# First three tiles' attention in float32, and the weights' words put together in PSUM

## The chip, the core and the metric

The kernel runs on one core of one Trainium2 chip. A core has five engines with a queue of instructions each: TensorE (PE) multiplies matrices, from SBUF into PSUM; VectorE (DVE), ScalarE (ACT) and GpSimd (POOL) work element by element; SyncE (SP) issues the DMA transfers between HBM and SBUF, and here also the DMA transposes within SBUF. Each engine's queue is laid down when the kernel is built, and an instruction waits on semaphores where it needs what another engine makes. The metric is the time on the device of one launch, in microseconds (us), lower is better.

## What is computed

A block of local and global attention, a gated feed-forward layer, and a soft mixture of eight experts, all on 3072 tokens. Inputs come as float32, except the weights `w_in` and `w_out` of the feed-forward layer, which the kernel receives as 64-bit words (float64) and turns into floating point of its own.

```python
scores = scale * np.matmul(q, k.transpose(0, 1, 3, 2))      # (4, 8, 768, 64)
keep = is_global | is_local                                  # 8 first keys, 96 last
scores = np.where(keep, scores + bias, -1e9)
a = softmax(scores)                                          # over the keys
x = np.matmul(a, v)           # -> (3072, 512)
h = x @ w_in                  # w_in (512, 2048)
x = (h * sigmoid(h)) @ w_out  # w_out (2048, 512)
...                           # soft mixture of experts on x, with phi, w1, w2
```

## The kernel before

The 3072 tokens are 24 tiles of 128, and three tiles make one of eight chunks. Precision is kept with float16 pairs: a float32 operand becomes a high part (`hi`, line 189) and a low part (`lo`, line 197), and a product takes three float16 matmuls, high by high, high by low and low by high. Making these parts is work for ScalarE, VectorE and GpSimd; strings such as `HE`, `PHE`, `PLE`, `L3E`, `LOE` say which engine makes which.

*Attention of a tile T.* `load` (line 240) brings q, k and v into a staging area; tiles 0 to 5 hold two heads on the 128 partitions (`paired`). `split` (line 247) makes the float16 parts of q, k and v; k and v go into rings of four tiles, `kr` and `v16`, and the global keys and values are kept in `kg` and `vg`. `s_step(T, pr)` (line 272) does the scores of two heads: the matmuls (line 293) into the banks `bS`, bias and row maximum on VectorE (line 298), exp on ScalarE (line 299). Every second step finishes half of the heads: the probabilities are split into two float16 parts (lines 312 and 313) and turned by a DMA transpose (line 314), or, for the last half of tile 2, turned by TensorE and split on the way out of PSUM (`flip`, line 208; string `PTE`). `pv_step` (line 324) multiplies them by v (line 336), divides by the row sums (line 346) and puts the transposed output into `xt`, the input of the feed-forward layer.

*Weights.* `w_ahead` (line 407) issues sixteen loads of 1 MB, eight for `w_in` and eight for `w_out`, each into a place (`place`) that is free, some held back by `GATE` until a certain half of the attention is done. `conv(p)` (line 414) turns such a piece into float16 parts, with the 64-bit word's low half as the place of the result. On VectorE line 421 takes the bits that show whether an exponent lies out of range; two TensorE matmuls with a one-column result (line 423) collect them in the bank `bM`. ScalarE (line 428) or GpSimd (line 426) turns one byte of the exponent into a 16-bit piece, VectorE adds the sign (line 429) and moves the fraction in (line 430). ScalarE makes the high part (line 440), and VectorE (line 448) or, for five pieces, ScalarE and GpSimd (lines 443 and 446) the low part. The staged place is then free for the next load.

*Feed-forward.* `l1_step(c, f)` (line 453) does a sixteenth of the hidden layer for chunk c: twelve matmuls (lines 460 to 462), tanh on ScalarE (line 464), the product on VectorE (line 466), and the two parts of the result. `l2_part` (line 475) does the second layer (lines 480 to 482), `l2_end` and `logits` what follows it. Both take their PSUM banks in turn from the four of `bW`.

*Order.* The program writes the attention of tiles 0 to 2 first (`first_items`), with conversion 0 after its fourth item (`START`). Then come the chunks: chunk 0 runs sixteen steps of the first layer, each pair of them behind one conversion of `w_in`, then eight conversions of `w_out`, each followed by its matmuls. Between these steps the attention of the next three tiles is put in (`other_items`), a share after each step. From this text a scheduler of the language makes each engine's queue, so that an operation can stand ahead of others that were written before it. Chunks 1 to 7 need no conversions.

Of the kernel before, what the change touches and what calls it, by code (L numbers as in the profile page):

```python
# [45 lines left out]
def p2(e):  # L46
    return float(2.0 ** e)
# [39 lines left out]
L3E = 'AAPPPAAAAAPAAAAA'  # L87
LOE = 'PVVPVVPVVPPVVVVV'
# [3 lines left out]
PTE = 'DDDDDA'  # L92
# [8 lines left out]
def fast_kernel(tc, keepp, q_l, k_l, v_l, q_f, k_f, n_global, n_local, w_in, w_out, phi, w1, w2, shapes, pick_c, out):  # L101
# [8 lines left out]
    with ExitStack() as ctx:  # L110
# [8 lines left out]
        bank = [psp.tile([128, 512], F32, name=f"bank{i}") for i in range(8)]  # L119
# [8 lines left out]
        one16 = ar.new([2], BF16)  # L128
# [53 lines left out]
        pt = [ar.new([2, 4, 2, 128], F16) for _ in range(2)]  # L182
        psum_ = [ar.new([H], F32) for _ in range(2)]
# [24 lines left out]
        def flip(hi_out, lo_out, in_, eng):  # L208

            for i in range(0, hi_out.shape[1], 4):  # L210
                tb = bW[flips[0] % 4]
# [27 lines left out]

        def load(T, bufs):  # L240
            if paired(T):
                bufs = [bufs[0][:, 0:4], bufs[1][:, 0:4], bufs[2]]
            for s, src in zip(bufs, (q_f, k_f, v_l) if paired(T) else (q_l, k_l, v_l)):
                nc.sync.dma_start(out=s, in_=src[T])
            staged[T] = bufs

        def split(T):
            qs, ks, vs = staged.pop(T)
# [3 lines left out]
            qd = q16[T % 2]  # L252
            n = 4 if paired(T) else 8
            if paired(T):
                qh, ql, qf = qd[:, 0:4], qd[:, 4:8], qs
            else:
                qh, ql, qf = qd, qd[64:128], qs[64:128]
            hi(he, qh, qs, E_QK)
            lo("P" if le == "P" else "V", ql, qf, E_QK, qh if paired(T) else ql)
            hi(he, kr[:, 0, 0:n, u], ks, E_QK)  # L260
            lo("V" if le == "V" else "P", kr[:, 1, 0:n, u], ks, E_QK, kr[:, 0, 0:n, u])
            v3 = vs.rearrange("p (h d) -> p h d", h=H)
            hi(he, v16[:, u, :, 0], v3, E_V)
            lo("V", v16[:, u, :, 1], v3, E_V, v16[:, u, :, 0])
            if t == 0:
                hi("P", kg[:, :, 0:n], kr[:, :, 0:n, u, 0:8], 0)
            if T == 0:
                hi("P", vg[0:8], v16[0:8, u], 0)
# [3 lines left out]
        def s_step(T, pr):  # L272
# [8 lines left out]
            if t == 0 and T < C0 and PTE[2 * T + half] != "D":  # L281
                pfb = pfb.rearrange("p h c -> p (h c)")[:, 0:512].rearrange("p (h c) -> p h c", h=4)
            qd = q16[T % 2]
            for i in range(2):
                h, r, terms = (pr, slice(64 * i, 64 * i + 64), ((0, 0), (0, 1), (1, 0))) if paired(T) else (2 * pr + i, slice(0, 128), ((0, 0), (0, 1)))
                for j, (y, z) in enumerate(terms):
# [938 lines left out]
```

## Time and profile before

| | |
|---|---|
| Median of 3 runs | 766.43 us (765.55 to 767.75) |
| The profiled execution | 765.0 us, of which the span of the profile is 763.2 us |
| TensorE busy | 683.0 us, 89% of the span |
| VectorE busy | 489.0 us, 64% |
| ScalarE busy | 336.6 us, 44% |
| GpSimd busy | 324.7 us, 43% |
| Mean granted TensorE clock | 0.964 |

All rows that follow come from that one profiled execution. A row of a group of instructions gives the line of the program, the engine, the operation, what it writes and reads, shapes and types, how many there are, then the busy time in us and the mean of one in ns, and then the idle time of the engine in front of them with what ended it. An instruction counts as busy from its start to its end, also where it is held up within. A line can be that of a helper: line 191 is any `hi` on ScalarE, lines 199 and 201 any `lo`. The names arena and rows are regions of SBUF, bank is PSUM.

### The profile page before, as it was taken

To read this page: it belongs to the slowest core of one execution; us is meant where nothing else is said; L and a number is where in the kernel's file an instruction comes from. 1 tells how busy PE (TensorE), PEld (TensorE's weight loads), DVE (VectorE), ACT (ScalarE), POOL (GpSimd) and SP (SyncE) were. 2 spreads that over 40 slices of the span, in tenths; PEclk is the share of its full clock that TensorE was granted. 3 is DMA by queue.
4 is the path that set the end of the run, shared out by engine and by line. 5 is a ranking of instruction groups with operands and counts; after the bars stand their busy time and mean duration, and the time that the engine had idled before them with its cause. 6 is when DMAs were issued, how large, how long until landed. Compare 5 with 4: busy or idle time off the path is not lost.

```text
span 763.2 us, 14337 instructions
## 1 busy us (share of the span) xinstructions
PE 683.0 (89%) x5559; PEld 395.0 (52%) x5559; DVE 489.0 (64%) x1108; ACT 336.6 (44%) x855; POOL 324.7 (43%) x267
## 2 busy tenths in 40 slices
PE   2477757598999999999999999999999999998995
PEld 1244423244655565556556654665466546665375
DVE  6999999997775487548735873597266306505232
ACT  7756786553552255245423542454156305303122
POOL 4689684733455356415633673337324320101000
PEclk9978969799999999999999999999999999999997
DMA  6787645565456355733563567354532694295987
GB/s 237 194 249 205 218 87 152 191 181 120 75 125 139 83 113 137 174 75 77 132 138 74 107 137 167 56 111 109 86 43 43 150 320 178 97 357 214 391 330 223
DMA packets 162747, 120.22 MB, mean 158 GB/s; under 512 B 137456, under 2 KB 147184, under 8 KB 156656
## 3 DMA queue, kind: packets, MB, share of 16 engines
q1 hardware_dynamic: 162672, 119.23, 58.4%
q8 instruction: 45, 0.74, 0.4%
q14 instruction: 30, 0.25, 0.1%
HBM read 79.10 MB, written 6.29 MB: 112 GB/s over the span
## 4 chain that ended last, share of the span: by engine, by line
PE 67%; DVE 16%; issue 5%; POOL 4%; DMA 4%; ACT 3%; SPq 0%; ACTq 0%; DVEq 0%; POOLq 0%
PE bank L480 8%; PE bank L481 8%; PE bank L482 8%; PE bank L460 8%; PE bank L462 8%; PE bank L461 8%; PE bank L293 4%; PE bank L336 3%; DVE arena L201 2%; DMA arena<-arena 2%; DVE arena L199 2%; POOL arena L193 2%; PE bank L864 2%; DVE arena L429 2%; PE bank L902 2%
## 5 line engine op out<-in xcount | busy, mean ns | idle before, releaser
L193 POOL TENSOR_SCALAR arena<-arena 128x1024 f16<-128x1024 f32 (+5 forms) x146 | 144.4, 1002 | 237.0 <-ACT arena L299 102.5
L460 PE MATMUL bank<-rows,arena 128*128 128x384 f16 x512 | 168.4, 330 | 6.2 <-ACT arena L191 4.0
L462 PE MATMUL bank<-rows,arena 128*128 128x384 f16 x512 | 168.3, 329 | 0.8 <-DVE arena L448 0.8
L461 PE MATMUL bank<-rows,arena 128*128 128x384 f16 x512 | 168.3, 329 | 0.0
L191 ACT ACTIVATE arena<-bank 128x384 f16<-128x384 f32 (+2 forms) x165 | 81.8, 505 | 177.0 <-DVE bank L466 98.7
L199 POOL TENSOR_TENSOR arena<-arena 128x1024 f16<-128x1024 f32 (+2 forms) x69 | 131.0, 1900 | 41.3 <-ACT arena L191 37.3
L299 ACT ACTIVATE arena<-arena 128x256 f32<-128x256 f32 (+1 forms) x192 | 92.2, 482 | 98.2 <-DVE arena L298 95.3
L481 PE MATMUL bank<-arena 128*128 128x512 f16 x336 | 128.9, 384 | 2.7 <-POOL arena L446 1.9
L480 PE MATMUL bank<-arena 128*128 128x512 f16 x336 | 129.1, 384 | 1.5 <-DVE arena L201 1.5
L482 PE MATMUL bank<-arena 128*128 128x512 f16 x336 | 128.7, 383 | 0.0
L201 DVE SCALAR_TENSOR_TENSOR arena<-bank,arena 128x384 f16<-128x384 f32 (+2 forms) x142 | 81.3, 572 | 32.7 <-ACT arena L191 32.0
L293 PE MATMUL bank<-arena 128*128 128x256 f16 (+3 forms) x432 | 63.4, 288 | 41.5 <-DVE arena L298 23.9
L298 DVE CUSTOM_DVE_ANT_0 arena<-bank,arena 128x256 f32<-128x256 f32 (+1 forms) x192 | 70.5, 395 | 44.2 <-PE bank L293 42.8
L466 DVE SCALAR_TENSOR_TENSOR bank<-arena,bank 128x384 f32<-128x384 f32 x128 | 71.2, 557 | 31.0 <-ACT arena L464 29.8
L199 DVE TENSOR_TENSOR arena<-arena 128x1024 f16<-128x1024 f32 (+2 forms) x50 | 74.7, 1496 | 12.6 <-POOL arena L193 12.2
L464 ACT ACTIVATE arena<-bank 128x384 f32<-128x384 f32 x128 | 61.9, 484 | 21.1 <-PE bank L462 20.8
L293 PEld LDWEIGHTS <-arena 128*128 128x128 f16 (+1 forms) x432 | 36.3, 101 | 66.5 <-issue 38.1
L462 PEld LDWEIGHTS <-arena 128*128 128x128 f16 x512 | 50.4, 99 | 35.4 <-issue 1.6
L461 PEld LDWEIGHTS <-arena 128*128 128x128 f16 x512 | 50.4, 98 | 34.5 <-issue 7.2
L460 PEld LDWEIGHTS <-arena 128*128 128x128 f16 x512 | 50.5, 99 | 31.4 <-issue 2.9
L482 PEld LDWEIGHTS <-arena 128*128 128x128 f16 x336 | 33.1, 99 | 43.9 <-issue 5.3
L480 PEld LDWEIGHTS <-arena 128*128 128x128 f16 x336 | 33.2, 99 | 38.1 <-issue 4.8
(174 smaller groups left out, 808.8 us busy)
## 6 DMA issues: line engine op xcount, KB each, us to landing
arena<-in_w_dram SPq DMA_DIRECT2D x31, 1024.0 KB, 7.4
arena<-in_q_l_dram SPq DMA_DIRECT2D x18, 512.0 KB, 3.7
arena<-in_k_l_dram SPq DMA_DIRECT2D x18, 512.0 KB, 4.0
arena<-in_w_in_dram SPq DMA_DIRECT2D x8, 1024.0 KB, 5.7
arena<-in_w_out_dram SPq DMA_DIRECT2D x8, 1024.0 KB, 4.9
arena<-in_v_l_dram SPq DMA_DIRECT2D x24, 256.0 KB, 3.0
out_dram<-arena SPq DMA_DIRECT2D x4, 768.0 KB, 7.6
out_dram<-arena SPq DMA_DIRECT2D x8, 384.0 KB, 5.0
```

Of the source, the lines that this page charges most:

```text
L191: A.activation(out=out, in_=in_, func=AF.Copy, scale=p2(e))
L193: G.tensor_scalar(out=out, in0=in_, scalar1=p2(e), scalar2=0.0, op0=ALU.mult, op1=ALU.add)
L199: (V if eng == "V" else G).tensor_tensor(out=out, in0=in_, in1=h, op=ALU.subtract)
L201: V.scalar_tensor_tensor(out=out, in0=in_, scalar=p2(e), in1=h, op0=ALU.mult, op1=ALU.subtract)
L293: mm(sp[i][:, :w] if t == 0 else sp[i].rearrange("p (s c) -> p s c", s=2), qd[r, 4 * y + h], kv, start=(j == 0), stop=(j == len(terms) - 1))
L299: A.activation(out=pw, in_=pw, func=AF.Exp, scale=-1.0, bias=nmx[:, T, h:h + 1], accum_out=psum_[T % 2][:, h:h + 1])
L460: mm(hp, wh, x[:, 0, k], start=(k == 0), stop=False)
L461: mm(hp, wh, x[:, 1, k], start=False, stop=False)
L462: mm(hp, wl, x[:, 0, k], start=False, stop=(k == 3))
L480: mm(op, gh, woh[:, f, 0], start=(f == 0), stop=False)
L481: mm(op, gh, woh[:, f, 1], start=False, stop=False)
L482: mm(op, gl, woh[:, f, 0], start=False, stop=(f == 15))
```

## The change

Six edits that belong together:

- Tiles 0 to 5 keep q and k as float32 (`kr32` and `q32` lie where the float16 parts lay). k is loaded in two halves of 64 columns straight into the ring, q into a buffer of its own. `split` no longer makes parts of q and k for these tiles, and each head's scores are one float32 matmul in place of three.
- Tiles 0 to 2 keep v as float32 too, and their probabilities: TensorE transposes these in blocks of 128, four to a bank, and ScalarE copies each bank to SBUF (`p32`). The output takes one float32 matmul a block. The DMA transposes of probabilities of these tiles are gone. Only tile 2's v and, for tile 0, eight rows of v are still split, for what later tiles read of them.
- Two banks of PSUM, one of the four of `bW` and `bM`, become one region `bC` of 1024 columns. In `conv` ScalarE writes the exponent's piece there as whole 32-bit words, for all sixteen pieces; VectorE puts sign and fraction in by two operations on it; ScalarE and VectorE take the two float16 parts from it, for all pieces.
- The exponent check's bits are gathered in SBUF by one VectorE operation a piece, and reduced at the end by two; the 32 matmuls are gone.
- The place of a raw piece counts as free, and the next load is issued, ahead of the two float16 parts.
- Chunk 0 takes its banks for both layers, and the transposes of tiles 0 to 2 theirs, from three of `bW`. The load of tile T + 2, for tile 5, is written after the last scores of tile 3.

The diff, cut to its core:

```diff
-L3E = 'AAPPPAAAAAPAAAAA'
-LOE = 'PVVPVVPVVPPVVVVV'
-PTE = 'DDDDDA'
+PTE = 'A'
-        bank = [psp.tile([128, 512], F32, name=f"bank{i}") for i in range(8)]
+        bank = [psp.tile([128, 512], F32, name=f"bank{i}") for i in range(6)]
+        bC = psp.tile([128, 1024], F32, name="words")
+        bank += [bC[:, 0:512], bC[:, 512:1024]]
...
         def load(T, bufs):
             if paired(T):
-                bufs = [bufs[0][:, 0:4], bufs[1][:, 0:4], bufs[2]]
+                nc.sync.dma_start(out=q_of(T), in_=q_f[T])
+                for z in range(2):
+                    nc.sync.dma_start(out=kr32[:, z, 0:4, T % NR], in_=k_f[T][:, :, 64 * z:64 * z + 64])
+                nc.sync.dma_start(out=v32[T].rearrange("p h d -> p (h d)") if T < C0 else v_next, in_=v_l[T])
+                return
...
             if paired(T):
-                qh, ql, qf = qd[:, 0:4], qd[:, 4:8], qs
+                v3 = v32[T] if T < C0 else v_next.rearrange("p (h d) -> p h d", h=H)
+                if T == 0:
+                    hi("P", kg32, kr32[:, 0, 0:4, u, 0:8], 0)
+                    hi("A", vg[0:8, :, 0], v3[0:8], E_V)
+                    lo("V", vg[0:8, :, 1], v3[0:8], E_V, vg[0:8, :, 0])
+                elif T >= C0 - 1:
+                    hi(he, v16[:, u, :, 0], v3, E_V)
+                    lo("V", v16[:, u, :, 1], v3, E_V, v16[:, u, :, 0])
...
+                if paired(T):
+                    r = slice(64 * i, 64 * i + 64)
...
+                    mm(so, q_of(T)[r, pr], kv, start=True, stop=True)
+                    continue
...
-                if T < C0 and PTE[2 * T + half] != "D":
-                    n = w // 32
-                    flip(ptb[:, 0:n], ptb[:, n:2 * n], pfb.rearrange("p h c -> p (h c)"), PTE[2 * T + half])
-                    held = ptb[:, 2 * n - 1, 127:128]
+                if T < C0:
+                    p32, src = pt32[half], pfb.rearrange("p h c -> p (h c)")
+                    for i in range(0, w // 32, 4):
+                        tb = bW[flips[0] % 3]
+                        flips[0] += 1
+                        for j in range(4):
+                            tr(tb[:, 128 * j:128 * j + 128], src[:, 128 * (i + j):128 * (i + j) + 128], ident)
+                        cp = PTE[flips[0] % len(PTE)]
+                        (A.copy if cp == "A" else V.tensor_copy)(out=p32[:, 128 * i:128 * i + 512], in_=tb)
...
+                if T < C0:
+                    nb = len(blocks)
+                    for s in range(nb):
+                        i = 128 * (nb * hh + s)
+                        mm(o[:, h], pt32[half][:, i:i + 128], v32[T - (nb - 1) + s][:, h], start=(s == 0), stop=(s == nb - 1))
+                    continue
...
-            V.tensor_scalar(out=odd16.bitcast(U16), in0=u16[:, :, 3], scalar1=0x7000, scalar2=0x3000, op0=ALU.bitwise_and, op1=ALU.bitwise_xor)
-            for j in range(2):
-                mm(bM[0:1], one16[:, 0:1], odd16[:, 512 * j:512 * j + 512], start=(p + j == 0), stop=(p + j == 16))
-            if L3E[p] == "P":
-                G.tensor_scalar(out=u16[:, :, 0], in0=by[:, :, 3], scalar1=1.0 / 32, scalar2=-0.484375, op0=ALU.mult, op1=ALU.add)
-            else:
-                A.activation(out=u16[:, :, 0], in_=by[:, :, 3], func=AF.Copy, scale=1.0 / 32, bias=-0.484375)
-            V.tensor_scalar(out=u16[:, :, 1], in0=u16[:, :, 3], scalar1=0x8000, scalar2=None, op0=ALU.bitwise_and)
-            V.scalar_tensor_tensor(out=low, in0=high, scalar=3, in1=low, op0=ALU.logical_shift_left, op1=ALU.bitwise_xor)
+            V.scalar_tensor_tensor(out=odd16, in0=u16[:, :, 3], scalar=0x3000, in1=odd16, op0=ALU.bitwise_xor, op1=ALU.bitwise_or)
+            word = bC.bitcast(I32)
+            A.activation(out=word, in_=by[:, :, 3], func=AF.Copy, scale=1.0 / 32, bias=-0.484375)
+            V.scalar_tensor_tensor(out=word, in0=high, scalar=-(2 ** 31), in1=word, op0=ALU.bitwise_and, op1=ALU.bitwise_xor)
+            V.scalar_tensor_tensor(out=word, in0=high, scalar=3, in1=word, op0=ALU.logical_shift_left, op1=ALU.bitwise_xor)
+            holder[place[p]] = None
+            w_ahead()
...
             A.activation(out=dst[0], in_=src, func=AF.Copy, scale=-p2(e - 128))
-            if LOE[p] != "V":
...
-            else:
-                V.scalar_tensor_tensor(out=dst[1], in0=src, scalar=-p2(e - 128), in1=dst[0], op0=ALU.mult, op1=ALU.subtract)
-            holder[place[p]] = None
-            w_ahead()
+            V.scalar_tensor_tensor(out=dst[1], in0=src, scalar=-p2(e - 128), in1=dst[0], op0=ALU.mult, op1=ALU.subtract)
...
-            hp = bW[turn[0] % 4][:, :n]
+            hp = bW[f % 3 if c == 0 else turn[0] % 4][:, :n]
...
-            op = bW[(turn[0] + m) % 4]
+            op = bW[(m + 1) % 3 if c == 0 else (turn[0] + m) % 4]
...
-                V.memset(odd, 0.0)
-                V.tensor_reduce(out=odd[0:1], in_=bM[0:1], axis=AX.X, op=ALU.max)
+                V.tensor_scalar(out=odd16, in0=odd16, scalar1=0x7000, scalar2=None, op0=ALU.bitwise_and)
+                V.tensor_reduce(out=odd, in_=odd16, axis=AX.X, op=ALU.max)
```

## Rows read from the trace of the kernel before

**Rows 1.** Busy by stretch: length, PE, PEld, DVE, ACT, POOL, clock, DMA share, GB/s

```profile
0.00:57.00 57.00, 29.02 (x237) 15.71 (x237) 48.28 (x115) 37.50 (x93) 37.24 (x43) 0.93 0.78 226
57.00:177.00 120.00, 86.86 (x553) 42.09 (x553) 116.62 (x149) 76.29 (x128) 77.77 (x48) 0.87 0.61 172
177.00:700.00 523.00, 515.49 (x4093) 303.98 (x4091) 302.92 (x787) 209.19 (x602) 206.13 (x171) 1.00 0.53 127
```

**Rows 2.** What VectorE waited for, 57 to 177 us: total, times, longest

```profile
DVE arena L298 <- POOL arena L193: 1.1, 1, 1.1
DVE arena L298 <- PE bank L293: 0.9, 1, 0.9
DVE arena L199 <- POOL arena L193: 0.7, 1, 0.7
```

**Rows 3.** Groups of VectorE by line and shape, 57 to 177 us

```profile
L430 DVE SCALAR_TENSOR_TENSOR arena<-arena 128x1024 int32<-128x1024 int32 x14 | 25.2, 1806 | 0.0
L429 DVE TENSOR_SCALAR arena<-arena 128x1024 uint16<-128x1024 uint16 x13 | 21.8, 1709 | 0.0
L448 DVE SCALAR_TENSOR_TENSOR arena<-arena 128x1024 f16<-128x1024 f32 x10 | 18.0, 1796 | 0.0
L421 DVE TENSOR_SCALAR arena<-arena 128x1024 uint16<-128x1024 uint16 x13 | 12.3, 945 | 0.0
L199 DVE TENSOR_TENSOR arena<-arena 128x1024 f16<-128x1024 f32 x6 | 11.9, 1991 | 0.7 <-POOL arena L193 0.7
...
L199 DVE TENSOR_TENSOR arena<-arena 128x512 f16<-128x512 f32 x3 | 2.0, 679 | 0.0
```

**Rows 4.** Single lines of VectorE, 0 to 190 us: shortest, median, longest in ns

```profile
L466 DVE SCALAR_TENSOR_TENSOR bank<-arena,bank x18: 547/549/556, 68.7 to 188.7; 128x384 f32<-128x384 f32 x18
L201 DVE SCALAR_TENSOR_TENSOR arena<-bank,arena x9: 543/546/692, 81.0 to 190.0; 128x384 f16<-128x384 f32 x6, 128x512 f16<-128x512 f32 x3
L430 DVE SCALAR_TENSOR_TENSOR arena<-arena x16: 1170/1770/4234, 23.4 to 170.4; 128x1024 int32<-128x1024 int32 x16
L429 DVE TENSOR_SCALAR arena<-arena x16: 1297/1525/3229, 21.8 to 168.7; 128x1024 uint16<-128x1024 uint16 x16
L421 DVE TENSOR_SCALAR arena<-arena x16: 643/690/2361, 16.2 to 174.7; 128x1024 uint16<-128x1024 uint16 x16
```

**Rows 5.** Groups of VectorE by line and shape, 0 to 57 us

```profile
L199 DVE TENSOR_TENSOR arena<-arena 128x512 f16<-128x512 f32 x7 | 6.9, 1012 | 0.1
...
L195 DVE TENSOR_SCALAR arena<-arena 128x512 f16<-128x512 f32 x3 | 3.8, 1279 | 0.0
...
L199 DVE TENSOR_TENSOR arena<-arena 128x1024 f16<-128x1024 f32 x2 | 2.4, 1214 | 0.0
```

**Rows 6.** Chain of work, 0 to 60 us: start us, us, what

```profile
28.92 2.61 DVE arena L201
...
32.73 5.53 DMA arena<-arena
```

**Rows 7.** Groups of ScalarE by line and shape, 0 to 177 us

```profile
L428 ACT ACTIVATE arena<-arena 128x1024 uint16<-128x1024 uint8 x12 | 30.0, 2499 | 0.4 <-DMA arena<-in_w_out_dram 0.4
...
L440 ACT ACTIVATE arena<-arena 128x1024 f16<-128x1024 f32 x16 | 18.4, 1148 | 28.1 <-DVE arena L430 26.5 <-DVE arena L448 1.6
```

**Rows 8.** Timeline of TensorE: start us, us, what (float16, then float32)

```profile
34.37 0.83 PE L293 MATMUL bank<-arena 64*128 64x256 f16 x6
...
732.98 1.13 PE L906 MATMUL bank<-arena 128*128 128x256 f32 x4
```

**Rows 9.** SP's queue, one issue; and the page's DMA issues, time to landing

```profile
2.14 0.43 SPq L244 DMA_DIRECT2D arena<-in_q_f_dram  x1
...
arena<-in_q_l_dram SPq DMA_DIRECT2D x18, 512.0 KB, 3.7
```

**Rows 10.** Line 440, once a round: its sixteen, and that of conversion 2

```profile
L440 ACT ACTIVATE arena<-arena x16: 1116/1145/1202, 25.3 to 172.7; 128x1024 f16<-128x1024 f32 x16
...
57.65 1.12 ACT L440 ACTIVATE arena<-arena 128x1024 f16<-128x1024 f32 x1
```

## What I predict

> **What bounds the kernel now.** I read the busy times of the engines by stretches of the span first [rows 1]. From 177 to 700 us TensorE is busy 515 of 523 us at full clock: whatever that train of matmuls starts earlier, the end comes earlier. So the question is what decides when it starts. Between 57 and 177 us VectorE is busy 116.6 of 120 us, TensorE 86.9, ScalarE 76.3 and GpSimd 77.8; between 0 and 57 us VectorE has 48.3, more than any other engine. The waits say the same: from 57 to 177 us VectorE waited 2.7 us in all [rows 2]. VectorE is the bound of the start-up, and what is taken off it there comes off the end unless a wait takes its place.
>
> What is VectorE doing? From 57 to 177 us the four lines that turn the weights' 64-bit words into two float16 parts (421, 429, 430, 448) take 12.3 + 21.8 + 25.2 + 18.0 = 77.3 us, two thirds of it [rows 3]. And they take longer than they need: line 430, with both inputs in SBUF, runs from 1.17 to 4.23 us for one shape, while line 466, whose second input and output lie in PSUM, takes 547 to 556 ns every time, in the same stretch and beside the same GpSimd [rows 4]. [...]
>
> **Part 1, the attention of the first three tiles (0 to 57 us).** Removed from VectorE: seven low parts of q and k, 6.9 us; three high parts of tile 1, 3.8; two low parts of tile 1's probabilities, 2.4; tile 1's low part of v, 2.6 (the piece at 28.92 us of the chain) [rows 5, 6]. That is 15.7 us. The three conversions that fall into this stage cost about as much after as before (part 2), so I leave them out. Five DMA transposes of probabilities go too; one stood in the chain with 5.5 us [rows 6]. In their place come forty TensorE transposes and ten ScalarE copies of 512 columns; a copy is about half of the 1.15 us that line 440 takes for 1024 [rows 7], together 5.8 us on an engine that is idle a third of this stage, and they replace float16 passes of like size there. TensorE computes each head's scores, and each block of the output, by one float32 matmul in place of three float16 ones. Float32 has a row elsewhere: line 906, four of 256 columns in 1.13 us, 0.28 us each; six float16 ones of line 293 take 0.83 us, three thus 0.42 [rows 8]. TensorE gains a little there and pays at most 40 x 0.28 = 11 us for the transposes, with 28 us free in this stage [rows 1].
>
> [...]
>
> How much of 15.7 us comes off the stage? VectorE is 85% busy in it, and the chain runs through these pieces and a DMA transpose besides. I take 16 us. Lower bound 8: scores, bias on VectorE, exp on ScalarE and transposes remain in sequence and become the limit. Upper bound 20: also most of a DMA transpose's latency. The keys come in two loads instead of one, in pieces of 256 bytes; on SP's queue that puts one more issue of 0.43 us [rows 9] ahead of tile 0's v, the identity and the loads behind: at nothing where other loads are under way, 1.3 us for three tiles without that cover. The load of tile 5 moves behind tile 3's last scores, whose buffer it overwrites; it has tile 4's scores to land, and without that cover it costs its landing, under the 3.7 us of a load twice as large [rows 9]. No DMA transpose stands between them on SP that was not there before.
>
> **Part 2, the conversion of the weights (57 to 177 us).** Each of sixteen rounds has on VectorE, after the change, one operation with two SBUF inputs (the bits for the exponent check) and three that work on the words in PSUM. The trace has no 1024-column one in PSUM: 384 columns take 0.549 us, 512 take 0.692 [rows 4], so 512 more at 1.11 ns are 0.57, together 1.26 us. The check's operation is like line 430: 1.17 us alone, 1.8 on average [rows 3, 4]; I take 1.5, since GpSimd's share in the conversion goes. Thirteen rounds lie in this stretch: 13 x (3 x 1.26 + 1.5) = 68.6 us in place of 77.3, a gain of 8.7 (4.9 to 13 for the check at 1.8 and 1.17). Three low parts of q and k of the next tiles give 2.0 more; the other operations with two SBUF inputs (line 199 at 1024 columns, 11.9 us for six, against 6 x 1.2 unstretched) may gain up to 4.7 from a quieter GpSimd, of which I count nothing [rows 3]. Sum: 10.7 us.
>
> [...]
>
> Against this stands a new wait. All rounds put their words together in one pair of banks, where before each worked in its own stretch of SBUF. So a round is a chain: ScalarE writes the exponents, two VectorE operations, ScalarE's high part, VectorE's low part, and only then the next round's write. The high part I price by line 440, 1.15 us. The write has two bounds [rows 7]: 2.5 us by line 428, which has the same input, and 1.15 by line 440, which moves as many whole words. I take 1.15, because on VectorE line 429, which also writes 16-bit pieces with gaps, takes at least 1.30 us where line 421, with the same input, writes densely in 0.64 [rows 4]: the gappy write is the likelier cause. The chain is then 1.15 + 2.52 + 1.15 + 1.26 = 6.1 us, or 7.4 with the dearer write. Before, a round came every (172.7 - 57.65) / 13 = 8.85 us [rows 10]; VectorE's work after is 8.85 - 10.7 / 13 = 8.0 a round. So VectorE stays the bound, but must have other work at hand twice a round; queued behind an operation that waits there are the attention's bias steps (ScalarE's exp waits for them) and line 466 (ScalarE's float16 parts and TensorE's next bank wait for it). Fully exposed the two waits are 2.3 us a round; covered they are nothing, as now. Other work is (116.6 - 77.3) / 13 = 3 us a round, and the check's 1.5, more than the 2.3; I take 0.6 us a round, 8 in all (0 to 20).
>
> **Off the path, at nothing.** The check's 32 matmuls leave TensorE, which is not the bound there. Three banks in place of four in chunk 0 bind only if one is held over two more steps; two steps come to a round of 8.85 us, and a bank's way (tanh, line 466, two ScalarE copies) is four operations of about 0.55. The raw words' place is free two operations earlier, and the next weight load with it: a gain if a load is late, which the 2.7 us of waits hardly show. The check's last masking and maximum (about 2 us) run beside the last matmuls of chunk 0. From 177 us on nothing changes.
>
> **Sum.** -16 - 10.7 + 8 = -18.7, say -19 us. The profiled execution took 765.0 us, of which the span is 763.2; the median is 1.4 us above it, so 766.4 - 19 = 747 us. The forecast's own range is 738 to 757.
>
> **Rivals.**
> - *The write is dear.* At 2.5 us the chain of 7.4 us and waits behind what runs on both engines (0.4 us at each of four handovers) make about 9 us a round, the old pace. The stretch gains nothing, the attention's 16 us lose a few: 754 us. For it: line 428 has the very input. Against: line 429.
> [...]
> - *Conversions drawn forward.* VectorE, freed early, does conversions during the attention, no wait is exposed and the quieter GpSimd helps: -16 - 10.7 - 4.7 = -31: 735 us.
> - *Slower: the single pair of banks.* If the waits lie open, with the dear write, a round is 8.0 + 2.5 + 1.15 = 11.7 us, 2.8 more than now, 13 x 2.8 = 37 us, less 16: 787 us. It decides from 8.85 + 16 / 13 = 10.1 us a round. For it: VectorE's order is fixed when the kernel is built, and everything behind a wait pays. Against: its queue finds other work nearly always now [rows 2].
> - *The same at 10.1 us a round*: no change, 766 us.
>
> **How the numbers follow.** Forecast 0.47, dear write 0.15, four passes 0.06, conversions forward 0.14, no change 0.06, slower 0.12. Faster by over 0.3% (2.3 us, about what a measurement can tell): 0.82; within it: 0.06; slower: 0.12. For 8 in 10 I leave out the slower case, most of the no-change case, and what lies below the best: 733 to 764.
>
> **What would show it.** Right: line 460's matmuls begin some 16 us earlier; operations on the words take 1.2 to 1.3 us without spread; ScalarE's exponent write is near 1.15 us; rounds are about 8.6 us apart; the train from 177 us on is unchanged, 19 us earlier. Wrong: VectorE waits for ScalarE more than 1 us a round; rounds over 10 us; TensorE full during the attention.

## The result, and the profile after

The changed kernel takes 777.45 us (median of 4 runs, 775.38 to 778.41), the kernel before beside it 765.99: a ratio of 1.0145, 95% interval 1.012 to 1.017. It is slower by 11.5 us, where I forecast 19 us faster. The profiled execution took 775.4 us, its span is 773.6.

The same stretches as in [rows 1], of the changed kernel (length, PE, PEld, DVE, ACT, POOL, clock, DMA share, GB/s):

```profile
0.00:57.00 57.00, 47.65 (x181) 35.15 (x182) 31.21 (x93) 30.15 (x84) 6.98 (x25) 1.00 0.63 198
57.00:177.00 120.00, 96.88 (x616) 49.46 (x617) 111.48 (x191) 73.50 (x168) 62.06 (x52) 0.90 0.64 176
177.00:700.00 523.00, 506.50 (x3964) 295.27 (x3963) 297.65 (x750) 201.63 (x567) 192.84 (x159) 0.99 0.52 125
```

The clock column counts time without a clock record as 1.00, and the trace has none before 62.1 us; more on this below. VectorE is relieved in the first 57 us as planned, by 17.1 us, but TensorE went from 29.0 to 47.7. And TensorE's train from 177 us on, which I took as untouched, has 9 us more holes. The matmuls of the attention, by line and shape, 0 to 57 us, of the changed kernel:

```profile
L374 PE MATMUL bank<-arena 128*128 128x64 f32 x80 | 19.2, 414 | 0.2 <-ACT arena L345 0.2
L311 PE MATMUL bank<-arena 64*128 64x256 f32 x37 | 15.7, 714 | 0.4 <-DVE arena L326 0.4
L343 PE MATMUL bank<-arena 128*128 128x128 f32 x40 | 12.0, 432 | 0.1
L311 PE MATMUL bank<-arena 64*128 64x128 f32 x16 | 3.8, 496 | 8.6 <-DMA arena<-in_k_f_dram 7.6 <-DVE arena L326 1.0
```

and of the kernel before:

```profile
L293 PE MATMUL bank<-arena 64*128 64x256 f16 x71 | 13.4, 381 | 9.8 <-DVE arena L298 9.0 <-POOL arena L193 0.8
L336 PE MATMUL bank<-arena 128*128 128x64 f16 x120 | 6.7, 232 | 1.8 <-DMA arena<-arena 1.8
```

The counts tell how to read a float32 row. Tile 0 has eight score matmuls of 128 columns, and there are 16 records; three tiles have 40 output matmuls, and there are 80 records; the 40 transposes have one each. Each of these float32 matmuls leaves two records. An output costs 19.2 / 40 = 0.48 us in place of 6.7 / 40 = 0.17 for its three float16 passes.

VectorE's and ScalarE's operations on the words, 0 to 190 us (shortest, median, longest in ns), which answer to [rows 4] and [rows 7]:

```profile
L470 ACT ACTIVATE words<-arena x16: 1085/1100/1142, 17.4 to 166.2; 128x1024 int32<-128x1024 uint8 x16
L471 DVE SCALAR_TENSOR_TENSOR words<-arena,words x16: 1209/1222/1229, 18.5 to 167.3; 128x1024 int32<-128x1024 int32 x16
L467 DVE SCALAR_TENSOR_TENSOR arena<-arena x16: 1206/1220/1781, 15.1 to 152.1; 128x1024 uint16<-128x1024 uint16 x16
L483 ACT ACTIVATE arena<-words x16: 1004/1023/1045, 23.3 to 170.3; 128x1024 f16<-128x1024 f32 x16
```

These came as forecast. A hole of TensorE's train in the middle of the span, from its timeline (start, us, what, in brackets the idle time and what ended it):

```profile
362.28 0.32 PE L495 MATMUL words<-rows,arena 128*128 128x384 f16 x1 [1.18 <-DVE arena L590]
```

A first-layer matmul into the region's first half waits for line 590, which reads a sum from the second half.

### The profile page after: what moved, and what is told of

It reads as the page before. It is cut to its first block, busy times and chain, and to the rows that moved or that the text cites. A ratio compares the mean times of both kernels' runs of the same rounds, so it can differ in the third digit from the quotient of the medians.

```text
span 773.6 us, 14119 instructions
## 1 busy us (share of the span) xinstructions
PE 711.2 (92%) x5471; PEld 414.7 (54%) x5471; DVE 464.1 (60%) x1095; ACT 320.2 (41%) x854; POOL 266.6 (34%) x244
## 4 chain that ended last, share of the span: by engine, by line
PE 68%; DVE 17%; ACT 5%; issue 3%; POOL 3%; DMA 2%; SPq 0%; ACTq 0%; DVEq 0%; POOLq 0%
PE bank L516 6%; PE bank L517 6%; PE bank L515 6%; PE bank L497 5%; PE bank L495 5%; PE bank L496 5%; DVE arena L209 3%; PE bank L311 3%; PE bank L321 2%; PE bank L374 2%; PE bank L378 2%; DVE arena L207 2%; PE bank L936 2%; PE words L516 2%; PE words L515 2%
## 5 line engine op out<-in xcount | busy, mean ns | idle before, releaser
L201 POOL TENSOR_SCALAR arena<-arena 128x1024 f16<-128x1024 f32 (+5 forms) x137 | 125.4, 927 | 291.6 <-ACT arena L327 121.5
L495 PE MATMUL bank<-rows,arena 128*128 128x384 f16 x400 | 133.3, 334 | 3.8 <-DVE arena L209 2.3
L497 PE MATMUL bank<-rows,arena 128*128 128x384 f16 x400 | 132.5, 332 | 1.8 <-DVE arena L484 1.8
L496 PE MATMUL bank<-rows,arena 128*128 128x384 f16 x400 | 133.3, 333 | 0.0
L207 POOL TENSOR_TENSOR arena<-arena 128x1024 f16<-128x1024 f32 (+2 forms) x64 | 117.4, 1836 | 36.5 <-ACT arena L199 32.1
L199 ACT ACTIVATE arena<-bank 128x384 f16<-128x384 f32 (+2 forms) x130 | 64.0, 504 | 120.0 <-DVE bank L501 65.6
L516 PE MATMUL bank<-arena 128*128 128x512 f16 x256 | 98.4, 384 | 4.1 <-DVE arena L484 4.1
L515 PE MATMUL bank<-arena 128*128 128x512 f16 x256 | 96.4, 387 | 5.1 <-ACT arena L483 5.1
L517 PE MATMUL bank<-arena 128*128 128x512 f16 x256 | 98.2, 384 | 0.0
L209 DVE SCALAR_TENSOR_TENSOR arena<-bank,arena 128x384 f16<-128x384 f32 (+1 forms) x107 | 61.5, 574 | 24.1 <-ACT arena L199 23.4
L501 DVE SCALAR_TENSOR_TENSOR bank<-arena,bank 128x384 f32<-128x384 f32 x100 | 55.8, 558 | 29.0 <-ACT arena L499 27.9
L497 PEld LDWEIGHTS <-arena 128*128 128x128 f16 x512 | 50.8, 99 | 37.3 <-issue 3.0
L496 PEld LDWEIGHTS <-arena 128*128 128x128 f16 x512 | 50.8, 99 | 35.8 <-issue 8.0
L495 PEld LDWEIGHTS <-arena 128*128 128x128 f16 x512 | 50.6, 99 | 34.6 <-issue 4.0
L207 DVE TENSOR_TENSOR arena<-arena 128x1024 f16<-128x1024 f32 (+1 forms) x38 | 55.0, 1448 | 14.5 <-POOL arena L201 14.0
L517 PEld LDWEIGHTS <-arena 128*128 128x128 f16 x336 | 33.1, 99 | 44.5 <-issue 6.5
L515 PEld LDWEIGHTS <-arena 128*128 128x128 f16 x336 | 33.1, 99 | 40.4 <-issue 7.5
L516 PEld LDWEIGHTS <-arena 128*128 128x128 f16 x336 | 33.2, 99 | 35.5 <-issue 1.7
L311 PE MATMUL bank<-arena 64*128 64x256 f32 (+1 forms) x96 | 31.1, 569 | 14.6 <-DMA arena<-in_k_f_dram 7.6
```

The lines of the kernel that those rows point to most:

```text
L199: A.activation(out=out, in_=in_, func=AF.Copy, scale=p2(e))
L201: G.tensor_scalar(out=out, in0=in_, scalar1=p2(e), scalar2=0.0, op0=ALU.mult, op1=ALU.add)
L207: (V if eng == "V" else G).tensor_tensor(out=out, in0=in_, in1=h, op=ALU.subtract)
L209: V.scalar_tensor_tensor(out=out, in0=in_, scalar=p2(e), in1=h, op0=ALU.mult, op1=ALU.subtract)
L495: mm(hp, wh, x[:, 0, k], start=(k == 0), stop=False)
L496: mm(hp, wh, x[:, 1, k], start=False, stop=False)
```

## The experiments

All in one table: where TensorE's timeline has the first matmul of the first layer, of chunk 2 and of chunk 7, the span of that execution, the median of all runs, and the ratio to the kernel before on the same chip. The first three columns cut the loss into stages.

| kernel | first layer | chunk 2 | chunk 7 | span | median | ratio, 95% interval |
|---|---|---|---|---|---|---|
| before | 57.8 | 256.9 | 630.0 | 763.2 | 766.0 to 767.7 | |
| changed | 57.9 | 256.4 | 634.1 | 773.6 | 777.5 | 1.0145, 1.012 to 1.017 |
| e1 attention | 60.3 | 259.8 | 632.2 | 767.1 | 769.6 | 1.0040, 1.0014 to 1.0065 |
| e2 words | 53.7 | 258.2 | 635.6 | 775.7 | 778.4 | 1.0157, 1.0106 to 1.0207 |
| e3 region only | 58.0 | 258.1 | 636.4 | 778.4 | 779.4 | 1.0151, 1.0107 to 1.0195 |
| e4 one pass | 45.1 | 243.7 | 623.7 | 762.0 | 764.8 | 0.9973, 0.9949 to 0.9998 |
| e5 returned | 57.4 | 254.4 | 627.0 | 760.7 | 764.1 | 0.9958, 0.9938 to 0.9979 |
| e6 returned, one pass | 44.6 | 241.9 | 614.8 | 748.6 | 752.6 | 0.9802, 0.9766 to 0.9839 |
| e7 words in place | 62.5 | 263.0 | 636.2 | 769.8 | 772.5 | 1.0070, 1.0049 to 1.0092 |
| e8 check twice | 59.4 | 270.7 | 643.4 | 776.9 | 778.7 | 1.0120, 1.0063 to 1.0177 |
| e9 scores one pass | 52.5 | 255.4 | 628.7 | 764.6 | 769.6 | 1.0040, 1.0018 to 1.0062 |
| e10 outputs one pass | 46.6 | 258.4 | 631.0 | 765.1 | 765.0 | 0.9970, 0.9954 to 0.9985 |
| e11 scores float16 | 64.2 | 264.6 | 637.9 | 773.1 | 773.7 | 1.0078, 1.0054 to 1.0101 |
| e12 check left out | 62.0 | 258.0 | 629.6 | 763.2 | 767.6 | 1.0018, 0.9998 to 1.0039 |
| e13 later tiles held | 57.4 | 250.6 | 625.8 | 760.1 | 759.7 | 0.9908, 0.9890 to 0.9925 |
| e14 held, unchecked | 62.1 | 247.9 | 620.4 | 755.1 | 757.3 | 0.9883, 0.9866 to 0.9901 |
| e15 check moved | 61.2 | 269.4 | 642.5 | 776.0 | 775.7 | 1.0114, 1.0097 to 1.0131 |
| e16 words returned | 54.0 | 258.2 | 630.3 | 763.8 | 767.7 | 1.0028, 1.0012 to 1.0045 |
| e17 before, held | 57.4 | 255.5 | 628.4 | 763.9 | 766.6 | 1.0010, 0.9995 to 1.0026 |
| e18 one pass, held | 44.4 | 238.8 | 612.1 | 747.1 | 747.9 | 0.9753, 0.9729 to 0.9777 |

### One part at a time

**e1** is the diff's attention edits with the old conversion, **e2** the rest with the old attention.

> The attention edits alone: float32 scores and outputs for the first tiles, with the conversion, the eight separate banks and the check by matmuls as in the kernel before. Theory (TensorE's price): a float32 matmul of 256 columns takes 0.57 us, not 0.28, so TensorE is full from 10 us to the first matmul of line 460's kind, which stays at 57 to 58 us, where it was; the 16 us forecast do not come. The time is then 766 within 3 us if nothing else moves, and the stretch from 57 us on looks like the kernel before. Rival (the attention edits carry the loss): the new reach of the attention's instructions is what puts gaps into the chunks after 180 us; then this kernel alone is at 772 to 778. Rival (hidden gain): the stage is shorter when the conversions are not on ScalarE and in the banks; first matmul near 45 us, time near 755.

> The words' edits alone: one region of 1024 columns, words put together there, check bits gathered in SBUF, three banks in turn for chunk 0; the attention of the first tiles in float16 as before. Theory: VectorE's 10 us of saved work in the conversion stage are used up by the chain through the one region, rounds come 8.5 to 9.0 us apart, chunk 0 ends 0 to 3 us earlier than in the kernel before, and chunks 1 to 7 and the stage behind them give 8 to 13 us back: 771 to 777. Rival (the loss is the attention's): this kernel keeps the gain of the ramp and nothing is given back: 760 to 765. Rival (the single pair of banks as forecast): rounds over 9.5 us, chunk 0 ends over 8 us later.

The attention alone costs 0.4%, with its first layer at 60.3 us where 57 to 58 were expected; the words alone cost the whole 1.6%, 1.4 us above the range of their theory. e2 loses little up to chunk 2 (1.3 us) and 4.3 more by chunk 7, 6.9 more behind. So the loss sits where no word is converted any more. **e3** leaves even the words out:

```diff
-        bank = [... for i in range(8)]
+        bank = [... for i in range(6)]
+        bC = psp.tile([128, 1024], F32, name="words")
+        bank += [bC[:, 0:512], bC[:, 512:1024]]
```

> The kernel before with one change: two of its eight banks are cut from one region of 1024 columns, as in the changed kernel; no instruction is added, taken away or changed. Theory (allocation): what one tile of two banks does to the order of the queues costs time after the ramp, without any work of the change: 769 to 776, with gaps in TensorE's train after 180 us and in the last stage. Rival (the edits' own work does it): 766 within 2 us.

779.4 us, above the theory's range: the whole loss, without one changed instruction. Its timeline has the same hole as the changed kernel's:

```profile
363.75 0.32 PE L462 MATMUL words<-rows,arena 128*128 128x384 f16 x1 [1.19 <-DVE arena L557]
```

Line 557 reads the other half. Reads and writes are tracked by region, so the fourth of the turning banks and the bank of the logits and slots, which have nothing to do with each other, now wait for each other. In the changed program as built 73 waits are of this kind, in e5's (next) none.

### The region given back

**e5** closes the region's pool after the last conversion:

```diff
...
+                words.close()
+                wp = ctx.enter_context(tc.tile_pool(name="back", bufs=1, space=PSUM))
+                for i in (6, 7):
+                    bank[i] = wp.tile([128, 512], F32, name=f"bank{i}")
+                bW[3] = bank[6]
+                bMs[0] = bank[7]
```

> The changed kernel, with the region of 1024 columns given back after the last conversion: from there on the two banks are two regions of 512 columns, as in the kernel before. Every instruction is that of the changed kernel. Theory (waits across the halves): in the changed kernel 73 waits tie a matmul into one half of the region, or a reader of one half, to the other half's user, and none of them here; the 6 us of gaps in chunks 1 to 6, and the 5 us lost behind the last chunk, go: 762 to 768, chunk 1 at 179 to 180 us as in the changed kernel, chunks 74.7 us apart. Rival (the loss after the ramp is the attention's order or the float32 work): 773 or more.

764.1: 13 us better than the changed kernel, and 0.4% faster than before. From chunk 2 to 7 it takes 372.6 us, as before (373.1), where the changed kernel takes 377.7 and e3 378.3. From chunk 7 to the end of the span it takes 133.7 us (before 133.2, changed 139.5, e3 142.0). **e16** does it to e2:

> As e2_words (the words' edits alone, the first tiles' attention in float16 as before), with the region given back after the last conversion. Theory: of e2_words' 11 us over the kernel before 8 to 10 go (its chunks and last stage lost 9.6), and the conversions' own gain of 2.7 us of the forecast is not reached: 767 to 771. Rival (forecast's term of conversions holds): 762 to 765.

767.7: of e2's 12 us 10 are gone, and what is left of the words' edits alone is 0.3% of loss, no gain.

### TensorE's price

**e4** (on the changed kernel) and **e6** (on e5) take one bfloat16 pass for each float32 matmul:

```diff
-                    mm(so, q_of(T)[r, pr], kv, start=True, stop=True)
+                    mm(so, b16(q_of(T)[r, pr]), b16(kv), start=True, stop=True)
```

and the same for the outputs; `b16` is a view of the upper half words.

> The changed kernel, with the scores of tiles 0 to 5 and the outputs of tiles 0 to 2 made from the upper 16 bits of their float32 operands alone, by one bfloat16 matmul each (the lower bits are left out); transposes and copies stay. Theory (TensorE's price): the score matmuls fall from 27 us to about 6 and the outputs from 19 to about 9 of the first 57 us, the first matmul of line 495 comes 12 to 18 us earlier than 57.9 us, and the time falls by about as much, to 760 to 766. Rival (the sequence of bias, exp, transpose and copy is the limit, TensorE only fills it): first matmul at 52 us or later, time 771 or more. Rival (the gain is given back behind the ramp): first matmul near 43 us, but the end of chunk 0 less than 5 us earlier, since the conversions' rounds set the pace from there; time 770 or more.

> As e5_returned, and with the one bfloat16 matmul of e4_one_pass in place of each float32 one (the lower 16 bits of the first tiles' operands are left out there). Theory: both losses taken away add up, 12 us of the ramp by TensorE's price and 11 behind it by the waits across the halves: 751 to 756, chunk 1 near 169 us. Rival (the earlier train runs into another limit, loads or the weights of the last stage): 759 or more.

Both as the theory had it: the first layer begins 12.8 us earlier in each, and the time falls by 12.6 and 11.5. In e6 the outputs take 3.3 us in place of 19.2.

VectorE had waited: the 31.0 us of work that it does before the first layer take it 44.6 us there, where the changed kernel's 31.2 take 57 (columns as in the first fence):

```profile
0.00:44.60 44.60, 25.23 (x121) 12.84 (x122) 30.99 (x102) 33.60 (x99) 11.02 (x28) 1.00 0.81 253
```

**e9**, **e10** split this, **e11** goes back to float16 scores only:

> As e5_returned, with only the score matmuls of tiles 0 to 5 made in one bfloat16 pass (their operands' lower 16 bits are left out); the outputs stay float32. Theory: the 12.5 us between e5_returned and e6_returned_one_pass are TensorE's, shared by busy time in the first 57 us: scores 19.5 of 38.7 us, outputs 19.2. This one then gives about half, 5 to 8 us: 756 to 760. Rival (the outputs, whose matmuls stand last in the chain to the first layer, carry it): under 3 us, 762 or more.

> As e5_returned, with only the output matmuls of tiles 0 to 2 made in one bfloat16 pass (lower 16 bits left out); the scores stay float32. Theory: the other half, 5 to 8 us: 756 to 760. Rival (the scores carry it): under 3 us, 762 or more.

> As e5_returned, with the scores of tiles 0 to 5 by three float16 passes on split q and k as in the kernel before (tile 1's high parts on ScalarE), and the outputs and transposes of tiles 0 to 2 in float32 as in the changed kernel; nothing is left out. Theory (TensorE and VectorE share the start): the scores cost TensorE 0.42 us a head in place of 0.57 to 0.65, some 6 us less in the first 57, and VectorE gets 4 to 5 us of low parts back there and 2 to 3 later; the start is 0 to 5 us shorter, the conversion stage 2 to 3 longer: 760 to 766. Rival (the split parts put VectorE and the copies back into the chain): first matmul of the first layer later than 57.4 us, 767 or more.

In all three the theory missed; e11 came out as its rival has it. The first layer starts 4.9 us earlier for the scores and 10.8 for the outputs, though their busy times are nearly equal (19.5 and 19.2 us in the changed kernel). But none of it reaches chunk 2, which begins 1.0 and 4.0 us later than in e5. e11's first layer starts 6.8 us later, its chunk 2 10.2. So an earlier first layer is not by itself an earlier end.

### VectorE's work in the conversions

**e7** puts the words together in SBUF in place (`word = low`), with eight separate banks and the place free after the low part again; **e8** writes the check's operation twice, **e12** for the first piece only.

> The changed kernel without the region: the words are put together in SBUF, in the staged low halves, eight separate banks; the same operations, the place free after the low part again. Theory (chain through the one region): a round has no predecessor to wait for, rounds come 7.5 to 8.3 us apart, chunk 1 at 168 to 173 us, time 752 to 760. Rival (stretched operations): the three operations of VectorE on the words take 1.5 to 2 us and the exponent write 1.2 to 2.5 in SBUF, a round has 9 us of VectorE, chunk 1 at 180 to 186 us, time 765 to 770.

> As e5_returned, with the check's operation on VectorE (1.29 us, outside the chain through the region) done twice in each conversion. Theory (the chain sets the pace): VectorE's waits of 1.0 to 1.5 us a round take most of it up, chunk 1 moves by less than 7 us, time at most 8 us over e5_returned. Rival (VectorE's work sets the pace, as the prediction had it): 13 rounds at 1.29 us are 17 us more at chunk 1 and in the time.

> As e5_returned, with the check's operation on VectorE done for the first piece only (the exponents of the other fifteen go unchecked). Theory (VectorE's work sets the pace of the conversions, as e8_check_twice indicates): 12 or 13 rounds lose 1.3 us each, 15 us: 747 to 752. Rival (at the changed kernel's 9.0 us a round the chain through the region is already near, and the loads): under 8 us, 756 or more.

e7 is 8.4 us slower than e5, at 772.5 above both of its ranges. The same operations with both inputs in SBUF, on VectorE, 0 to 200 us:

```profile
L480 DVE SCALAR_TENSOR_TENSOR arena<-arena 128x1024 f16<-128x1024 f32 x16 | 23.8, 1493 | 0.0
L469 DVE SCALAR_TENSOR_TENSOR arena<-arena 128x1024 int32<-128x1024 int32 x16 | 23.4, 1462 | 0.9 <-ACT arena L468 0.9
L464 DVE SCALAR_TENSOR_TENSOR arena<-arena 128x1024 uint16<-128x1024 uint16 x16 | 21.7, 1354 | 0.0
L470 DVE SCALAR_TENSOR_TENSOR arena<-arena 128x1024 int32<-128x1024 int32 x16 | 20.7, 1294 | 0.0
```

89.6 us, where the changed kernel's four take 20.7 + 19.6 + 19.5 + 19.5 = 79.3. The stretch that I read from [rows 4] is real, and PSUM takes it away: the changed kernel's lines 471, 472 and 484 take 1.21 to 1.24 us each time, where e7's three (lines 469, 470 and 480) average 1.29 to 1.49. That e7's time comes from it is not shown: its rounds are 8.4 us apart, against 8.9 in e5 (from the third high part to the last), and its first layer starts 5.1 us later. e8's second operation, 16 x 1.41 = 22.6 us of VectorE, cost 14.6. That is nearer to the rival's 17 than to the theory's 8 at most and speaks for VectorE's work, but e15 below loses nearly as much by order alone. And e12's 19 us less gave nothing (767.6). What filled the freed time? VectorE's bias operations (line 298 of the kernel before) 0 to 185 us, of e12 (shortest, median, longest in ns):

```profile
L327 DVE CUSTOM_DVE_ANT_0 arena<-bank,arena x80: 272/415/427, 8.5 to 182.3; 128x256 f32<-128x256 f32 x64, 128x128 f32<-128x128 f32 x16
```

80 heads, against 55 before and 70 in e5: attention of later tiles was drawn forward by the scheduler. And TensorE stood before their outputs; its waits in e12, 57 to 200 us (total, times, longest):

```profile
PE bank L379 <- DMA arena<-arena: 15.3, 7, 3.7
```

### The later tiles held back

**e13** (on e5) and **e14** (on e12) hold tile 7's scores until the last conversion is through, with an operation that changes no value:

```diff
+            if T == 7 and pr == 0:
+                x = q16[T % 2][:, 0, 0:1]
+                V.scalar_tensor_tensor(out=x, in0=last[0], scalar=0.0, in1=x, op0=ALU.mult, op1=ALU.add)
...
```

(`last[0]` is a column of the last conversion's low part.) **e15** only writes e5's check operation behind the two operations on the words.

> As e5_returned, with the scores of tile 7 held back by data until the last conversion is through (one tiny VectorE operation, which changes no value). In e5_returned 70 heads' bias operations have run by 185 us, 56 in the kernel before. Theory (later attention drawn forward takes VectorE and makes TensorE's queue wait for transposes): fewer than 65 heads by 185 us, chunk 2 begins 2 to 6 us earlier than 254.4, 758 to 763. Rival (it is only work done earlier that comes off later): within 2 us of e5_returned, 762 to 766.

> As e12_check_left_out (fifteen pieces unchecked), with tile 7 held back as in e13_later_tiles_held. In e12_check_left_out 80 heads have run by 185 us, and TensorE stood 15 us before output matmuls that wait for a DMA transpose. Theory: with them held back VectorE's freed time goes to the conversions: under 66 heads by 185 us, chunk 2 begins at 240 to 250 us in place of 258, 750 to 758. Rival (another limit: chain through the region, loads): 763 or more.

> As e5_returned, with the same instructions; only the check's operation is written behind the two operations on the words in place of ahead of them. Theory (the queues' order alone is worth several us in this stage): it differs from e5_returned by 3 us or more, either way. Rival (order is worth little, the work decides): within 2 us, 762 to 766.

e13: 62 heads by 185 us, 759.7, as its theory had it. e14: 757.3, 10 us better than e12, and TensorE's wait of 15.3 us is 4.4 (e14, the same view):

```profile
PE bank L384 <- DMA arena<-arena: 4.4, 3, 2.1
```

Against e13, though, the check's 19 us are worth only some 2. There VectorE waits for ScalarE on the words; its waits in e14, 57 to 200 us:

```profile
DVE words L478 <- ACT words L477: 4.0, 5, 1.2
DVE arena L491 <- ACT arena L490: 3.8, 4, 1.1
```

7.8 us, where e13 has 1.5 of them: with less to do VectorE meets the chain through the region. And e15 is 11.6 us slower than e5 with the same instructions: their order alone is worth as much as any part of the change.

**e17** holds tile 7 in the kernel before; **e18** is e13 with e6's one pass.

> The kernel before with tile 7 held back until the last conversion is through, as in e13_later_tiles_held, and nothing of the change. Theory (the change's freed VectorE time is what tile 7 is drawn into): the kernel before runs only 56 heads by 185 us anyway, so it stays within 2 us of the kernel before: 764 to 768. Rival (the gain of e13 is holding back, not the change): 758 to 762.

> As e13_later_tiles_held, with the scores of tiles 0 to 5 and the outputs of tiles 0 to 2 in one bfloat16 pass as in e6_returned_one_pass (lower 16 bits left out). Theory: TensorE's price of float32 is 11 to 13 us with tile 7 held back too: 746 to 750. Rival (the two gains are the same time): 752 or more.

e17: no change, so holding tile 7 back is worth nothing without the change. e18: 747.9; TensorE's price is 11.8 us here as well. With nothing left out, e13 is the fastest version, 0.9% below the kernel before and 2.3% below the changed one.

## Why the prediction was wrong, point by point

**"From 177 us on nothing changes"** is the step that turned the sign. The diff shows two banks becoming slices of one region, and I asked of it only whether conversions wait for each other. Both slices have users after the conversions. Measured: 11.7 us (e3 over the kernel before) and 13.4 (the changed kernel over e5).

**The attention stage, -16 us**, came to nothing. The step that failed is TensorE's price, in three places.

First, I read the four records of line 906 [rows 8] as four matmuls; they are two, so float32 costs 0.57 us for 256 columns there, not 0.28.

Second, line 906 runs at 733 us under a granted clock of 1.00, and the start does not. The 0.93 of [rows 1] and the 1.00 above count unrecorded time as full; the traces' clock records begin at 42.7 us (before) and 62.1 us (changed), and have two levels, 1.00 and 0.50. The same four records, the scores of two heads, show both levels in the changed kernel, the second row in a stretch recorded at 1.00:

```profile
54.57 1.23 PE L311 MATMUL bank<-arena 64*128 64x256 f32 x4
...
74.20 0.70 PE L311 MATMUL bank<-arena 64*128 64x256 f32 x4
```

One head alone takes 1.22 us at 109.67 us, where 0.50 is recorded, and 1.22 in the start too (33.90 us). So the changed kernel's start ran at the lower level, and so did the start before (float16 outputs begin 0.053 us apart up to 39.5 us, as they do at 113.6 us under a recorded 0.50; at 44.5 us, under a recorded 1.00, it is 0.029). I had set a float32 row of the upper level against a float16 row of the lower. Two heads whose records start together take 1.23 us there, hardly more than one alone. On average a head's scores of 256 columns cost 15.7 / 18.5 = 0.85 us in the first 57, before 13.4 / 23.7 = 0.57. The outputs, for which I took no row at all, are the larger part: 0.48 against 0.17 us, 12.5 us over forty.

Third, and visible without any new row: I set 11 us for the transposes (they took 12.0) against "28 us free in this stage", free in a stage of 57 us. In the stage of 41 us that I forecast, TensorE's 29 + 11 = 40 us left nothing for the 7.6 us in which it waits for the first keys (the row of 128 columns above). The cover has to be measured in the shortened stage.

A TensorE that is full during the attention stands in the prediction as a sign against it, and the chances have "four passes" at 0.06. No run shows how many passes a float32 matmul takes. What the runs show is its price: 11.5 to 12.6 us (e4, e6, e18), against a single bfloat16 matmul. For 256 columns at a granted clock of 1.00 line 906's 0.57 us is 3.8 times the 0.15 of a float16 matmul of line 293 (four in 0.60 us, at 273.01 us). For the outputs it is more: 0.48 against 0.17 / 3 = 0.056, 8.6 times (24 of the 120 float16 ones at the upper level, all others at the lower).

The rest of that term held in the main: once TensorE's price is gone the first layer begins 12.8 us earlier, of the 16.

**The conversion's own terms were right in size.** Operations on the words 1.22 us (1.26 taken), without spread; the check 1.29 (1.5); the exponent write 1.10 (1.15, so the dear write is out); high part 1.02 (1.15). The check's last masking and maximum, set at about 2, take 0.41 + 1.21 = 1.62 (lines 835 and 836). The 0.4 us for each of four handovers, in the rival with the dear write, was an estimate that no row shows; in the changed kernel the medians of the sixteen rounds, from line 470 over 471, 472 and 483 to 484, are 0.46, 1.11, 0.04 and 0.63. Per round VectorE does 79.3 / 16 = 4.96 us, forecast 5.28, before 5.95. The rounds, 9.0 us apart, were forecast at 8.6, before 8.85. VectorE's waits from 57 to 177 us rose from 2.7 us [rows 2] to 8.3, by 5.6 where I took 8, but they are other waits than those I priced. Only 0.4 us stands on the words (line 484), where ScalarE waits instead: 16.0 us in front of line 483 and 8.6 in front of line 470, 0 to 190 us. VectorE's longest lies in the first layer, behind tanh (57 to 177 us; total, times, longest):

```profile
DVE bank L501 <- ACT arena L499: 4.2, 3, 3.8
...
DVE arena L484 <- ACT arena L483: 0.4, 1, 0.4
```

Operations with one input in SBUF are stretched too: lines 421 and 429 run from 0.64 to 2.36 and from 1.30 to 3.23 us [rows 4]; lines 466 and 471, which ran evenly (0.547 to 0.556 us before, 1.209 to 1.229 in the changed kernel), have their other operand in PSUM. Beside the stretched ones the trace before has GpSimd at work: of line 430's sixteen the five with none of its operations beside them take 1.17 to 1.24 us, the eleven others 1.52 to 4.23.

The sum of -10.7 + 8 = -2.7 us stood for this stage; chunk 2 begins 0.5 us earlier than before in the changed kernel and 2.5 earlier in e5. That agreement is luck in the main: the rounds did not get shorter, e15 shows that an order of the same work moves this stage by 15 us, and e16 that the words by themselves gain nothing. The gain that I looked for went partly into later tiles' attention (70 heads by 185 us, not 55), which fits that chunk 2 begins 3.8 us earlier still with tile 7 held back (e13).

**The rival for slower**, rounds of over 10.1 us through the single pair of banks, was the wrong mechanism: rounds stayed near 9 us. The single region did make the kernel slower, but after the conversions.

**What stays open.** Rounds come 8.1 to 9.3 us apart in e5, e6, e8, e12, e13 and e14, with from 3.7 to 6.4 us of VectorE's conversion work in each. Which of the three queues sets that pace changes from kernel to kernel, and I can't say why e9 and e10 lost their earlier start. Their granted clock from 57 to 120 us is lower, 0.83 and 0.86 against e5's 0.89. In e10 that is a part of it at most, by an estimate under 2 us of TensorE's time (0.03 of 63 us); it was not tested. No run separates, in TensorE's price, what float32 itself costs from the lower level of the clock. Nor do the runs separate, in e3's 11.7 us, the false waits themselves from the other order that the scheduler chose because of them.

## What to carry to other kernels

When two buffers become one region, list every later user of either half: they wait for each other from then on, also where the region's purpose is long over; give it back when it has served. Measure the cover that hides new work in the stage as it will be, not as it is. Count one matmul's records by a line whose number of matmuls is known, and price work by a row at the clock at which it will run; where no clock is on record, the spacing of equal matmuls shows the level (0.053 and 0.029 us here). And where a scheduler lays down the queues, freed time goes to whatever it finds ready: a saving needs something that keeps later work from taking it, and a forecast needs a margin for the order alone, here some 12 us.

## What the hardware showed that I had not expected

A float32 output matmul of 64 columns takes 0.25 us at the upper level of the clock and 0.45 at the lower: in e9 four of them (eight records) take 1.79 us at 25.68 us and 1.00 at 27.53, on either side of its first clock record at 27.3 us (1.00); eight take 3.52 us at 51.12 us in the changed kernel, 0.44 each. 256 columns take 0.57 at the upper level (line 906), so a quarter of the columns costs 0.44 of the time. ScalarE's high part of 1024 columns takes 1.02 us from PSUM, 1.145 from SBUF [rows 10]. And the exponent write, 2.50 us into 16-bit pieces with gaps [rows 7], takes 1.10 as whole words into PSUM from the same input, and 1.15 as whole words with gaps in SBUF (e7).
